# Moving every large on-chip buffer to a multiple of 512 bytes, with six stream slots set at six different offsets

## The chip, the cores and the metric

The kernel runs on one core of a Trainium2 chip. The metric is the device time of one execution in microseconds. Three runs of the kernel before took 1680.58, 1680.69 and 1686.5 us; their median is 1680.69 us.

## The reference

Attention in chunks of 64 tokens, then two feed-forward layers over the same 4608 tokens of width 512, all in float32:

```
scores = scale * (q_c @ k_c.T) ; attn = softmax(scores) ; x = attn @ v_c     # 8 x 8 x 9 chunks of 64 x 64
xn = x / sqrt(mean(x*x) + 1e-6) * rms_g
y  = (silu(xn @ w_gate) * (xn @ w_val)) @ w_out                              # 512 -> 1536 -> 512
h  = y @ w_in ;  out = (h * clip(h + 3, 0, 6) / 6) @ w_out2                  # 512 -> 2048 -> 512
```

## The kernel before

The tokens are cut into nine blocks of 512. Each value that TensorE multiplies is held as two float32r parts, a high one and a low one, and each product is three matmuls (high by high, low by high, high by low), each of a 128x128 stationary operand and a moving operand of 512 columns. Most blocks are taken in pairs with seven products in place of eight (Strassen's scheme), whose sums of operands are made once on the chip and kept in HBM.

The order of the work is written out by hand in each engine's program. There are four parts, in order of time: the start, with the attention of the first block and the preparation of the first weights; the first layer for blocks 0 to 2, one by one (`mm_up`, `mm_down_a`), with attention of later blocks spread among it (to about 360 us); the first layer for three pairs of blocks (`product` at L1032 with tiles `xu` and `wo`, `mm_down_a` with `gs` and `wd`; to about 910 us); and the second layer, one block alone and then four pairs (`product` with `xo` and `wq`, `product_down` at L1582 with `gs` and `wq`; to the end).

The operands of the second layer come from HBM through class `Stream`: 240 tiles `wq` of 128 x 1024 float32, 512 KB each, go in turn into six slots, the tags "q", "k", "qT", "kT", "p" and "v" of pool `at`. Each such tile is the stationary operand of 12 matmuls. Earlier in the kernel the same six slots hold the tiles of the attention (`Half` and `Pair`).

On-chip memory is laid out by pools in the order in which they are opened, and within a pool by tags in the order of their first use; each buffer is rounded up to 32 bytes. Before pool `const` lie 1152 bytes. Pool `const` holds `ident`, `ones`, `ones_r` (512 bytes of each partition each) and three small tiles, and ends at byte 2784. So pool `wp` (36 buffers of 4096 bytes, with weights, moving operands and results) starts at byte 2784, which is 224 past a multiple of 512. All pools after it up to `at` hold buffers of 2048, 4096 or 8192 bytes, so each of these starts 224 bytes past a multiple of 512 as well, the six slots of `at` among them. Small tiles come last, in `sm`: maxima, sums, and the tags "r" (one value of each partition, the root of the mean square) and "rc" (16 values). Each tag of `sm` has four buffers in turn.

A tile that is allocated again waits until the readers and the writer of its old content are done; the framework puts these waits on the engine that writes the new content.

The lines that matter below: L1032 in `product`, L1582 in `product_down`, L1021 in `mm_up`, L1046 to L1049 in `mm_down_a`, L1054 to L1058 in `mm_down_b`, L1782 (the last product), L656 in `heat` (matmuls of 256 columns that keep TensorE busy in the start), L650 in `pad` (64 columns), L926 in `Wide.scores` (64 columns, float32), L626 and L630 in `root` and `table`, L633 and L635 in `inv`.

Of the kernel before, what the change touches and what calls it, by code (L numbers as in the profile page):

```python
# [10 lines left out]
F32 = mybir.dt.float32  # L11
# [63 lines left out]
def fused_kernel(  # L75
# [25 lines left out]

    NQ = FB // 2
    const = ctx.enter_context(tc.tile_pool(name="const", bufs=1))
    wp = ctx.enter_context(tc.tile_pool(name="wp", bufs=36))
    xn_p = ctx.enter_context(tc.tile_pool(name="xn", bufs=1))
    xf_p = ctx.enter_context(tc.tile_pool(name="xf", bufs=1))
# [5 lines left out]
    at_p = ctx.enter_context(tc.tile_pool(name="at", bufs=1))  # L112
    sm_p = ctx.enter_context(tc.tile_pool(name="sm", bufs=4))
# [6 lines left out]
    eps = const.tile([128, 1], F32, name="eps")  # L120
    three = const.tile([128, 1], F32, name="three")
    g_sb = const.tile([128, KD], F32, name="g_sb")
    PS = ps_p.tile([128, 8, 512], F32, name="PS")
    yd = [dr_p.tile([128, KD, N], F32, name=f"yd{b}") for b in range(NB)]
    ATT, GB, VB, YB = 0, 2, 3, 4


    def w_src(kind, f):
# [370 lines left out]
    class Att:  # L499
# [22 lines left out]
        def trans_qk(self):  # L522
            ps = PS[:, self.bank:self.bank + 2, :]
            for z, t in ((0, self.q), (1, self.k)):
                if z > 0 and self.i in (0, 2):
                    self.pad()
                for a in range(NP):
                    nc.tensor.transpose(ps[:, z, a * 128:(a + 1) * 128], t[:, a * 128:(a + 1) * 128], ident)
            self.qT, self.kT = self.bufs("qT", "kT")

        def out_q(self):
            nc.scalar.copy(self.qT, PS[:, self.bank, :])

        def out_k(self):
            nc.scalar.copy(self.kT, PS[:, self.bank + 1, :])

        def scores(self):
            self.s = PS[:, self.bank:self.bank + 2, 0:256]
            ps = self.s.rearrange("p z (e c k) -> p z e c k", e=2, c=2)
            qT = self.qT.rearrange("p (a t) -> p a t", a=NP)  # L540
            kT = self.kT.rearrange("p (a t) -> p a t", a=NP)
            for a, c, j in FOURS:
                x = side(a, j)
                nc.tensor.matmul(
                    ps[x * 64:(x + 1) * 64, a // 2, a % 2, c, :],
                    qT[j * 64:(j + 1) * 64, a, c * 64:(c + 1) * 64],
                    kT[j * 64:(j + 1) * 64, a, c * 64:(c + 1) * 64],
                    start=True,
                    stop=True,
                )  # L550
# [28 lines left out]
        def trans_p(self):  # L579
            for a in range(NP):  # L580
                nc.tensor.transpose(
                    PS[:, self.bank, a * 128:(a + 1) * 128], self.p[:, a * 128:(a + 1) * 128], ident
                )
            self.pT, self.sq = self.bufs("pT", "sq")

        def out_p(self):
            nc.scalar.copy(self.pT, PS[:, self.bank, :])

# [33 lines left out]
                )  # L622

        def root(self):
            self.r = sm_p.tile([128, 1], F32, tag="r", name="r")
            nc.scalar.activation(self.r, self.ms, AF.Sqrt, scale=1.0 / DM, bias=eps)  # L626

        def table(self):
            t = sm_p.tile([128, 1], F32, tag="r", name="rt")
            nc.scalar.activation(t, eps, AF.Sqrt)  # L630

        def inv(self):
            nc.vector.reciprocal(self.r, self.r)  # L633
            self.dg = self.sq[:, 384:512]
            nc.vector.tensor_scalar(self.dg, ident, self.r, None, op0=ALU.mult)  # L635
# [310 lines left out]
    class Rms:  # L946
# [17 lines left out]

        def inv(self):
            t = at_p.tile([128, N], F32, tag="p", name="rT")
            r = sm_p.tile([128, 16], F32, tag="rc", name="rc")
            nc.vector.transpose(out=t, in_=self.rt)
            nc.vector.reciprocal(r, t.rearrange("p (j n) -> p j n", n=32)[:, :, 0])
            nc.vector.transpose(  # L970
                out=self.rt.rearrange("p (j n) -> p j n", n=32),
                in_=r.rearrange("p (j o) -> p j o", o=1).to_broadcast([128, 16, 32]),
            )
# [140 lines left out]
    with tc.manual_schedule():  # L1114
# [247 lines left out]
        for p in range(3):  # L1362
# [4 lines left out]
            def gt(f, z):  # L1367
                key = ("x", 0) if z == 0 and f < 4 else (z, f // 2)
                if key not in g:
                    g[key] = (  # L1370
                        xn_p.tile([128, KD, N], F32, tag="XL", name="ge")
                        if key == ("x", 0)
                        else wp.tile([128, 2, N], F32, tag="w", name="gu")
                    )
                return g[key][:, f % 4 if key == ("x", 0) else f % 2, :]
# [6 lines left out]
            for i in range(NI + 1):  # L1382
# [13 lines left out]
                for n, (pr, m) in enumerate(slots):  # L1396
# [19 lines left out]
                    elif (pr, m) == (3, 0):  # L1416
                        t = gt(h0, 1)
                        vec(t, t, bank(4, 0), ALU.add)
                        later = t
                    elif (pr, m) == (4, 1):  # L1420
                        t = gt(h1, 0)
# [3 lines left out]
                    elif (pr, m) == (3, 1):  # L1425
                        s = hold.pop("s2")
                        vec(s, s, bank(4, 1), ALU.add)
                        t = gt(h0, 1)
# [8 lines left out]
                    elif (pr, m) == (2, 1):  # L1437
                        t = gt(f0, 0)
                        vec(t, t, bank(0, 1), ALU.mult)
                    elif (pr, m) == (7, 0):  # L1440
                        t = gt(f1, 1)
# [3 lines left out]
                    elif (pr, m) == (7, 1):  # L1445
# [3 lines left out]
                        t = gt(f1, 1)  # L1449
# [103 lines left out]
        def slot(i, name):  # L1553

            key = (i, name)
            if key not in G:
                if i < 2 and name != "t":
                    t = xn_p.tile([128, KD, N], F32, tag=("XH", "XL")[i], name="gx")
                    names = ("11", "12", "21", "22")
                elif name == "t":  # L1560
                    t = wp.tile([128, 2, N], F32, tag="w", name="gt")
                    names = ()
                else:
                    t = wp.tile([128, 2, N], F32, tag="w", name="gu")
                    names = ("11", "12") if name[0] == "1" else ("21", "22")
                for n, x in enumerate(names):
                    G[i, x] = t[:, n, :]
                if not names:
                    for n in range(2):
                        G[i - i % 2 + n, "t"] = t[:, n, :]  # L1570
            return G[key]
# [81 lines left out]
        for b in range(1, NB, 2):  # L1653
# [7 lines left out]
            for I in range(NG + 1):  # L1661
# [7 lines left out]
                for pr, m in slots:  # L1669
# [20 lines left out]
                    elif pr == 3:  # L1690
                        t = slot(i, "12")
# [7 lines left out]
                    elif pr == 7:  # L1699
                        t = slot(i, "22")  # L1700
# [124 lines left out]
```

## Time and profile before

| | |
|---|---|
| median of three runs | 1680.69 us |
| profiled execution, its own time | 1683.83 us |
| its span, first to last instruction | 1682.0 us |
| TensorE busy | 1650.1 us (98%) |
| VectorE, ScalarE, GpSimd busy | 1086.3, 845.0, 458.7 us |
| mean granted TensorE clock | 0.994 |
| HBM traffic | 222 GB/s over the span |

The profile is of one execution, which took 3.1 us more than the median of the three runs. TensorE is busy almost throughout. A "busy" matmul lasts about 389 ns in the trace, since matmuls overlap; what one costs in a dense stretch is the stretch divided by its matmuls.

### The profile page before, as it was taken

To read this page: it belongs to the slowest core of one execution; us is meant where nothing else is said; L and a number is where in the kernel's file an instruction comes from. 1 tells how busy PE (TensorE), PEld (TensorE's weight loads), DVE (VectorE), ACT (ScalarE), POOL (GpSimd) and SP (SyncE) were. 2 spreads that over 40 slices of the span, in tenths; PEclk is the share of its full clock that TensorE was granted. 3 is DMA by queue.
4 is the path that set the end of the run, shared out by engine and by line. 5 is a ranking of instruction groups with operands and counts; after the bars stand their busy time and mean duration, and the time that the engine had idled before them with its cause. 6 is when DMAs were issued, how large, how long until landed. Compare 5 with 4: busy or idle time off the path is not lost.

```text
span 1682.0 us, 26541 instructions
## 1 busy us (share of the span) xinstructions
PE 1650.1 (98%) x9920; PEld 1352.1 (80%) x9920; DVE 1086.3 (65%) x1600; ACT 845.0 (50%) x1409; POOL 458.7 (27%) x336
## 2 busy tenths in 40 slices
PE   8999999999999999999999999999999999999998
PEld 7777788878878878788887888888788878887886
DVE  7998566656565775758436378448746764874475
ACT  6785344455454454545434344455445544654552
POOL 1001434322226522264226622131023003301310
PEclk9999999999999999999999999999999999999999
DMA  9923777748887598945979766667866786777665
GB/s 276 279 53 77 202 207 225 209 142 251 293 262 222 167 296 277 301 164 188 365 240 317 291 238 225 213 190 249 219 210 222 209 241 198 218 229 225 193 200 139
DMA packets 336096, 375.07 MB, mean 223 GB/s; under 512 B 184288, under 2 KB 260064, under 8 KB 335840
## 3 DMA queue, kind: packets, MB, share of 16 engines
q1 hardware_dynamic: 273984, 302.84, 59.6%
q10 hardware_dynamic: 61984, 70.53, 12.5%
q8 instruction: 79, 1.29, 0.3%
q14 instruction: 49, 0.40, 0.1%
HBM read 292.55 MB, written 80.74 MB: 222 GB/s over the span
## 4 chain that ended last, share of the span: by engine, by line
PE 77%; DVE 11%; DMA 5%; ACT 3%; issue 2%; SPq 2%; POOL 0%; ACTq 0%; DVEq 0%; POOLq 0%
PE PS L1032 35%; PE PS L1582 13%; PE PS L1021 9%; PE PS L1046 5%; PE PS L1049 5%; PE PS L1047 5%; DMA wo<-ops 2%; DVE gs L1576 1%; PE PS L853 1%; DVE wtmp L183 1%; DVE gt L1718 1%; PE PS L926 1%; DMA sraw<-in_moe_w_out_dram 1%; PE PS L1054 1%; PE PS L1055 1%
## 5 line engine op out<-in xcount | busy, mean ns | idle before, releaser
L1032 PE MATMUL PS<-xu,wo 128*128 128x512 f32 x1512 | 353.8, 393 | 4.8 <-DVE gu L1360 2.3
L1032 PEld LDWEIGHTS PS<-xu,wo 128*128 128x128 f32 x1512 | 283.3, 189 | 66.5 <-DVE gu L1360 3.2
L1032 PE MATMUL PS<-xo,wq 128*128 128x512 f32 x1344 | 305.3, 389 | 0.0
L1582 PE MATMUL PS<-gs,wq 128*128 128x512 f32 x1296 | 296.2, 390 | 2.4 <-DVE gs L1576 2.1
L1032 PEld LDWEIGHTS PS<-xo,wq 128*128 128x128 f32 x1344 | 252.3, 188 | 52.4
L1582 PEld LDWEIGHTS PS<-gs,wq 128*128 128x128 f32 x1296 | 242.7, 188 | 55.3 <-DVE gs L1576 5.0
L1021 PE MATMUL PS<-XH,w 128*128 128x512 f32 x576 | 149.1, 401 | 6.8 <-ACT sg L1329 4.5
L1021 PEld LDWEIGHTS PS<-XH,w 128*128 128x128 f32 x576 | 107.8, 191 | 30.7 <-ACT sg L1329 5.2
L1046 PE MATMUL PS<-gs,wd 128*128 128x512 f32 x288 | 113.4, 394 | 1.6 <-DVE gu L1360 1.6
L1047 PE MATMUL PS<-gs,wd 128*128 128x512 f32 x288 | 112.2, 389 | 0.0
L1077 POOL TENSOR_TENSOR al<-sg,ah 128x512 fp32r<-128x512 f32 x40 | 56.1, 1403 | 156.3 <-ACT ah L1075 152.1
L1356 POOL TENSOR_TENSOR gs<-gu,gs 128x512 fp32r<-128x512 f32 x60 | 86.6, 1462 | 42.4 <-ACT gs L1355 35.3
L1360 DVE TENSOR_TENSOR gu<-gu,PS 128x512 f32<-128x512 f32 x60 | 41.0, 685 | 82.2 <-ACT gu L1442 42.2
L1649 POOL TENSOR_TENSOR gt<-gx 128x512 f32<-128x512 f32 x8 | 10.3, 1289 | 299.8 <-DVE gx L1646 299.8
L1576 DVE TENSOR_TENSOR gs<-gu,gs 128x512 fp32r<-128x512 f32 x88 | 67.9, 792 | 30.9 <-ACT gs L1575 30.6
L1575 ACT CAST gs<-gt 128x512 fp32r<-128x512 f32 x96 | 58.4, 623 | 50.1 <-DVE gt L1718 44.7
L1513 DVE SCALAR_TENSOR_TENSOR gu<-gu,PS 128x512 f32<-128x512 f32 x48 | 32.8, 684 | 72.6 <-ACT gu L1510 72.6
L1021 PE MATMUL PS<-XL,w 128*128 128x512 f32 x288 | 78.2, 394 | 0.0
L1075 ACT CAST ah<-sg 128x512 fp32r<-128x512 f32 x52 | 32.3, 621 | 89.9 <-DVE sg L1333 58.0
L1049 PE MATMUL PS<-gs,wd 128*128 128x512 f32 x288 | 77.0, 389 | 0.0
L1575 ACT CAST gs<-gu 128x512 fp32r<-128x512 f32 x96 | 57.2, 621 | 22.6 <-DVE gs L1576 15.6
L1649 POOL TENSOR_TENSOR gt<-gu 128x512 f32<-128x512 f32 x24 | 32.5, 1355 | 129.1 <-DVE gu L1646 124.9
(251 smaller groups left out, 2888.9 us busy)
## 6 DMA issues: line engine op xcount, KB each, us to landing
wq<-stash_in SPq DMA_DIRECT2D x128, 512.0 KB
wo<-ops SPq DMA_DIRECT2D x126, 512.0 KB
wq<-sums_out SPq DMA_DIRECT2D x64, 512.0 KB
wq<-stash_out SPq DMA_DIRECT2D x48, 512.0 KB
wd<-keep_out SPq DMA_DIRECT2D x36, 512.0 KB
yd<-yst SPq DMA_DIRECT2D x18, 512.0 KB
ops<-w ACTq DMA_DIRECT2D x36, 256.0 KB
v<-in_v_dram SPq DMA_DIRECT2D x32, 256.0 KB
```

Source lines behind the costliest of these rows:

```text
L1021: nc.tensor.matmul(ps, w(wi, c), xs[c][xi], start=(i == 0), stop=(i == n - 1))
L1032: nc.tensor.matmul(PS[:, bank, :], op[:, wi, c * 128:(c + 1) * 128], x[xi][:, c, :], start=first and i == 0, stop=last and i == 5, skip_gr ...
L1046: nc.tensor.matmul(ps, wm[0], a[0], start=first, stop=False)
L1047: nc.tensor.matmul(ps, wm[1], a[0], start=False, stop=False)
L1049: nc.tensor.matmul(PS[:, banks[m], :], w[:, 0, m * 128:(m + 1) * 128], a[1], start=False, stop=last)
L1077: nc.gpsimd.tensor_tensor(lo, t, hi.bitcast(F32), op=ALU.subtract)
L1356: nc.gpsimd.tensor_tensor(w[:, 1, :], t, w[:, 0, :].bitcast(F32), op=ALU.subtract)
L1360: nc.vector.tensor_tensor(o, x, y, op=op)
L1575: nc.scalar.copy(w[:, 0, :], x)
L1576: e.tensor_tensor(w[:, 1, :], x, w[:, 0, :].bitcast(F32), op=ALU.subtract)
L1582: nc.tensor.matmul(PS[:, banks[m], :], op[:, wi, m * 128:(m + 1) * 128], x[xi], start=first and (wi, xi) == (0, 0), stop=False, skip_group ...
L1649: nc.gpsimd.tensor_tensor(slot(i, "t"), slot(i, "12"), slot(i, "11"), op=ALU.subtract)
```

## The change

Three edits. A tile `gap` of 24 float32 is put behind `g_sb` in `const`, and a pool `few` with two buffers a tag stands between `const` and `wp` and takes the tags "r" and "rc" from `sm`. With these, `few` starts at byte 2880 and `wp` at byte 3072, a multiple of 512. The pools after it follow: every buffer from `wp` to `tmp` now starts at a multiple of 512, where it started 224 bytes past one. Last, the six tags of `at` are touched once ahead of the program, in a fixed order, with tiles of 32 or 64 bytes between them, so that the slots "q", "k", "qT", "kT", "p", "v" start 0, 32, 64, 128, 192 and 224 bytes past a multiple of 512.

```
     const = ctx.enter_context(tc.tile_pool(name="const", bufs=1))
+    few_p = ctx.enter_context(tc.tile_pool(name="few", bufs=2))
     wp = ctx.enter_context(tc.tile_pool(name="wp", bufs=36))
...
     g_sb = const.tile([128, KD], F32, name="g_sb")
+    const.tile([128, 24], F32, name="gap")
     PS = ps_p.tile([128, 8, 512], F32, name="PS")
...
+    for n, (tag, gap) in enumerate((("q", 8), ("k", 8), ("qT", 16), ("kT", 16), ("p", 8), ("v", 0))):
+        at_p.tile([128, 2 * 512], F32, tag=tag, name=tag)
+        if gap:
+            at_p.tile([128, gap], F32, tag=f"gap{n}", name="gap")
...
         def root(self):
-            self.r = sm_p.tile([128, 1], F32, tag="r", name="r")
+            self.r = few_p.tile([128, 1], F32, tag="r", name="r")
...
         def table(self):
-            t = sm_p.tile([128, 1], F32, tag="r", name="rt")
+            t = few_p.tile([128, 1], F32, tag="r", name="rt")
...
-            r = sm_p.tile([128, 16], F32, tag="rc", name="rc")
+            r = few_p.tile([128, 16], F32, tag="rc", name="rc")
```

The touched tiles and the gaps have no instruction. On every engine the instructions are the same ones in the same order as before, with other addresses. The only waits that differ are on ScalarE in the start, where the four tiles `r` now share two buffers with `rt`. Before, ScalarE's rows there (`r` is the root of one group of 128 tokens, `xf` and `XH` hold the first block's tokens):

```order
L626 ACTIVATE r<-PS,eps 128x1 [waits PE_49]
L612 COPY xf<-PS 128x2x4x64 [waits PE_49]
L615 ACTIVATE pT<-PS 128x2x4x64
L194 CAST w<-wraw 128x512 [waits DVE_49]
L626 ACTIVATE r<-PS,eps 128x1 [waits PE_49]
L659 CAST XH<-xf 128x4x128 [waits DVE_49,Activation_49]
L626 ACTIVATE r<-PS,eps 128x1 [waits PE_49,Activation_49]
```

The same rows of ScalarE after the change (each line number is 7 higher):

```order
L633 ACTIVATE r<-PS,eps 128x1 [waits PE_49,Activation_49]
L619 COPY xf<-PS 128x2x4x64 [waits PE_49]
L622 ACTIVATE pT<-PS 128x2x4x64
L201 CAST w<-wraw 128x512 [waits DVE_49]
L633 ACTIVATE r<-PS,eps 128x1 [waits DVE_49,PE_49]
L666 CAST XH<-xf 128x4x128 [waits DVE_49]
L633 ACTIVATE r<-PS,eps 128x1 [waits PE_49]
```

Nothing moved. The second root now also waits for ScalarE's own write to `rt`, and the third for VectorE's last reading of the first root, since each takes over a buffer.

## Rows read from the trace of the kernel before

**Rows 1.** The page: busy time of the engines, DMA's share, the chain by engine.
```profile
PE 1650.1 (98%) x9920; PEld 1352.1 (80%) x9920; DVE 1086.3 (65%) x1600; ACT 845.0 (50%) x1409; POOL 458.7 (27%) x336
...
DMA packets 336096, 375.07 MB, mean 223 GB/s; under 512 B 184288, under 2 KB 260064, under 8 KB 335840
...
PE 77%; DVE 11%; DMA 5%; ACT 3%; issue 2%; SPq 2%; POOL 0%; ACTq 0%; DVEq 0%; POOLq 0%
```

**Rows 2.** Chain that ended last, by pieces: start us, us, what.
```profile
441.44 16.55 PE PS L1032 x72
...
489.02 4.93 PE PS L1032 x11
...
1058.88 76.16 PE PS L1032 x336
...
1135.04 54.19 PE PS L1582 x239
```

**Rows 3.** Busy time by stretches: us, engines (instructions), granted clock, DMA share, GB/s.
```profile
441.50:457.90 16.40, 16.40 (x73) 13.52 (x74) 10.77 (x14) 9.89 (x14) 6.13 (x4) 1.00 0.96 354
1059.00:1135.00 76.00, 76.00 (x337) 62.96 (x336) 31.84 (x47) 36.74 (x60) 20.63 (x16) 1.00 0.66 203
...
487.00:493.70 6.70, 6.70 (x76) 5.58 (x76) 2.00 (x2) 1.75 (x3) 0.76 (x1) 0.50 0.72 233
```

**Rows 4.** Groups of matmuls: count, then busy us, mean ns, idle before.
```profile
L1032 PE MATMUL PS<-xu,wo 128*128 128x512 f32 x1512 | 353.8, 393 | 4.8 <-DVE gu L1360 2.3 <-ACT gu L1442 1.1 <-DVE s L1360 0.9
L1032 PE MATMUL PS<-xo,wq 128*128 128x512 f32 x1344 | 305.3, 389 | 0.0
L1582 PE MATMUL PS<-gs,wq 128*128 128x512 f32 x1296 | 296.2, 390 | 2.4 <-DVE gs L1576 2.1
L1021 PE MATMUL PS<-XH,w 128*128 128x512 f32 x576 | 149.1, 401 | 6.8 <-ACT sg L1329 4.5 <-ACT XH L659 2.2
...
L1021 PE MATMUL PS<-XL,w 128*128 128x512 f32 x288 | 78.2, 394 | 0.0
L1049 PE MATMUL PS<-gs,wd 128*128 128x512 f32 x288 | 77.0, 389 | 0.0
...
L1021 PE MATMUL PS<-xr,wq 128*128 128x512 f32 x192 | 46.0, 389 | 0.0
L1049 PE MATMUL PS<-al,w 128*128 128x512 f32 x144 | 38.5, 389 | 0.0
...
L1058 PE MATMUL PS<-w,al 128*128 128x512 f32 x64 | 17.1, 389 | 0.0
L1782 PE MATMUL PS<-gs,wq 128*128 128x512 f32 x48 | 13.2, 434 | 2.5 <-DMA wq<-stash_out 2.5
```

**Rows 5.** What TensorE waited for: us in total, times, longest.
```profile
PE PS L1021 <- ACT sg L1329: 4.5, 2, 3.2
PE PS L596 <- ACT pT L587: 2.8, 6, 0.7
PE PS L1782 <- DMA wq<-stash_out: 2.5, 1, 2.5
PE PS L1032 <- DVE gu L1360: 2.3, 1, 2.3
```

**Rows 6.** Chain again: two runs of 64-column matmuls.
```profile
6.19 1.07 PE PS L650 x16
...
397.09 1.09 PE PS L926 x64
```

**Rows 7.** DMA queues, 1188.4 to 1192.4 us: packets, MB, share of 16 engines.
```profile
q1 hardware_dynamic: 3851, 0.48, 81.4%
```

**Rows 8.** DMA queues, 400 to 420 us: packets, MB, share of 16 engines.
```profile
q1 hardware_dynamic: 1373, 4.49, 72.4%
q10 hardware_dynamic: 544, 0.52, 7.5%
```

**Rows 9.** ScalarE and VectorE in order of time: start us, us, instruction.
```profile
24.47 0.20 ACT L630 ACTIVATE rt<-eps 128x1 f32<-128x1 f32 x1
...
27.58 0.31 ACT L626 ACTIVATE r<-PS,eps 128x1 f32<-128x1 f32 x1
...
29.72 0.27 ACT L626 ACTIVATE r<-PS,eps 128x1 f32<-128x1 f32 x1
...
27.46 0.29 DVE L635 TENSOR_SCALAR pT<-ident,r 128x128 f32<-128x128 f32 x1
```

## The prediction

> **What bounds the kernel now.** I read the page first. TensorE is busy for 1650.1 of 1682.0 us, and 77% of the chain that ended last is TensorE's own work [rows 1]. The list of its waits then shows that what is not busy is small: its longest entries are 4.5, 2.8, 2.5 and 2.3 us [rows 5], and all its gaps together are 1682.0 - 1650.1 = 31.9 us. So a change pays only if it changes what one matmul costs, or adds or takes a good part of those 32 us.
>
> Next, the pieces of the chain, for the cost of one matmul. In the second layer 336 matmuls of L1032 take 76.16 us without a break: 226.67 ns each. A piece that follows other work carries a lead of about 0.23 us (16.55 us for 72, less 72 x 226.67 ns = 16.32 us) [rows 2]. L1582, with other tiles, gives 54.19 / 239 = 226.7 ns [rows 2]. So the cost is one number all over the kernel. Once the clock is at the lower level (granted 0.50, which is 1.2 GHz) [rows 3]: there 11 matmuls take 4.93 us, less the lead 4.70 us or 427 ns each [rows 2]. 512 columns at 1.2 GHz are 426.7 ns, so nothing is added at that level. At 2.4 GHz they are 213.33 ns, and the row says 226.67: every matmul carries 13.33 ns beyond its columns. I call it the bubble.
>
> How many matmuls carry it? The groups of 512 columns [rows 4] are 1512 + 1344 + 1296 + 576 + 288 + 192 + 48, plus L1046, L1047 and L1049 with 288 (`gs`) and 144 (`ah`, `al`) each and L1054, L1055 and L1058 with 64 each (of these triples the last stands for all): 6,744. The bubble is 6,744 x 13.33 ns = 89.9 us of the run. It is the only sizable thing that an address could touch.
>
> **The change part by part.** It removes and adds no instruction. Three things differ.
>
> *The new waits.* The second root (27.58 us) waits for ScalarE's own write to `rt`, over at 24.47 + 0.20 = 24.67 us. The third (29.72 us) waits for VectorE's last reading of the first root, over at 27.46 + 0.29 = 27.75 us, 1.97 us earlier [rows 9]. Cost 0; the cover is those 1.97 us. Were it gone, the cast of `XH` and the last root stand behind that root on ScalarE, and the first matmuls of the first layer wait for them. To cost 1 us the reading would have to be 3 us late. The tag "rc" is used by VectorE alone, in order: 0.
>
> *Transfers.* Buffers move from 224 bytes past a multiple of 512 to 0, and the six slots to 0, 32, 64, 128, 192, 224. In a stretch of only small packets, 3,851 packets of 125 bytes use 81.4% of 16 engines over 4.0 us: 0.814 x 16 x 4000 / 3851 = 13.5 ns each [rows 7]. The stores on q10 between 400 and 420 us are 956 bytes each and take 0.075 x 16 x 20000 / 544 = 44.1 ns; the loads on q1 there are 3,270 bytes and take 168.7 ns [rows 8]. The first two give 30.6 ns for 831 bytes, or 0.0368 ns a byte, and 13.5 - 125 x 0.0368 = 8.9 ns that every packet pays. All of these touch buffers at 224, so no row separates a part due to the address. Bounds: at best all 8.9 ns of a 168.7 ns load goes, 5.3%; the chain is on DMAs for 5% of 1682 us = 84 us [rows 1], so this gives -4.5 us. At worst packets lengthen by as much: a landing late by 5.3% costs +4.5 us in the earlier parts, and nothing in the second layer, where 336 and 239 matmuls run through without a wait for a tile [rows 2] at a DMA share of 0.66 [rows 3]. I take 0, since start 224 is present in every row from 125 to 3,270 bytes and the same 8.9 ns fits them without an address.
>
> *The matmuls.* Moving and stationary operands both start 224 bytes past a multiple of 512 now. After, the moving ones start at 0, stationary `w`, `wo`, `wd` and `gs` at 0, and `wq` at one of six offsets. No row of before shows another start for a 512-column matmul. The nearest rows are the 64-column runs: L650 reads `ones` for both operands, 128 bytes past a multiple of 512, and L926 reads `qT` and `kT`, 224 past one. 16 of the first take 1.07 us; 64 of the second, which run four side by side in the array (so 16 passes), take 1.09 us [rows 6]. That is 67 and 68 ns a pass: no price for the start. They are float32 and pass at a slower rate, so they don't settle it. Bounds for one 512-column matmul: 213.33 ns from below, what its columns need; from above one more bubble, 240 ns. I take 226.67, the value of every dense piece, because a fixed cost of each matmul that the lower clock hides needs no address to explain it.
>
> Between engines, one rule bears on this. The Trainium skill, "SBUF — State Buffer", section "SBUF: two separate sides", says that DMA ports and engine ports are apart and that TensorE and ScalarE never wait on another user of the memory. Here the trace agrees: at a DMA share of 0.96 the 72 matmuls from 441.44 us cost the same as the 336 at 0.66 [rows 2, 3]. By that rule no placement of the slots against the transfers can change the matmuls, and the sum stays at 0.
>
> VectorE, ScalarE and GpSimd read and write the moved buffers too. No row shows a price by address for them. TensorE's waits for them are a part of 31.9 us, so even 10% on all their operations is at most 3 us either way.
>
> **The sum.** 0 + 0 + 0. The profiled execution took 1683.83 us, its span 1682.0; the three runs' median of 1680.69 lies 3.1 us below. Against the median I forecast 1680.5 us. Adding the small bounds (4.5 and 3 us each way), the likeliest case lies between 1673 and 1688 us. A measurement of this kernel tells no less than 0.5%, 8.4 us, from no change.
>
> **The rivals.**
>
> *A: the bubble comes from where the moving operand starts.* Then it goes everywhere, since all moving operands now start at 0: 1680.7 - 89.9 = 1591 us. For it: 13.33 ns at 4 bytes a column is the time of 32 columns, or 128 bytes, the size of a piece that is read too much when the start is odd; and it is hidden at the lower clock, as a reading cost would be. Against it: the 64-column rows. Chance 0.06. The Trainium skill, "TensorE: Matmul & The Clock Gate", section "Wait — 56ns, not 53.3ns?", gives N/2.4 GHz plus about 2.5 ns back to back, 215.8 ns for 512 columns. The trace disagrees by 10.9 ns a matmul; by that rule, as an estimate, 73 us of the bubble is a loss of this kernel, and rival A would end near 1607 us.
>
> *B: the bubble comes from both operands starting at the same place*, so that the reading of the next stationary operand and of the moving one collide. It would go where they differ: in the second layer, 1344 + 1296 + 192 + 48 = 2,880 matmuls (12 a tile, 240 tiles), for the five slots of six that are not at 0: 2,400 x 13.33 ns = 32.0 us, 1649 us. If only some offsets help, 6.4 us for each such slot. For it: all dense rows have equal starts and all have the bubble. Against it: the reading of a 128-column operand is a quarter as long as that of 512 columns, and a collision would not cost exactly the same in 336 and in 239 matmuls with different tiles. Chance 0.11, a third of it for one to three slots.
>
> *C: slower.* Unequal starts are what collides, and equal starts are the free case. The place is the second layer; the price is one more bubble on 2,400 matmuls, +32 us, 1713 us; it decides from 8.4 us / 2,400 = 3.5 ns a matmul. One bad slot costs 6.4 us, two 12.8. For it: before, no dense matmul has unequal starts, so it is untried. Against it: the same row that speaks against B. Chance 0.10, half of it for one or two slots.
>
> *D: the shift does less than it says*, since the slots also serve the attention, whose tiles are written in pieces; there only the transfers could feel it, and that is in the bounds above.
>
> **How the numbers follow.** No effect 0.73, A 0.06, B 0.11, C 0.10. The time is that of the first, 1680.5 us. Its own range is 1673 to 1688. To leave out no more than 2 in 10, the range goes to 1660 below (three slots of B) and 1695 above (two slots of C); outside are A, two thirds of B and half of C, 0.18. Faster by over 0.5%: A and most of B, 0.16. Slower: C without its single-slot case, and a little for transfers, 0.10. Within: 0.74.
>
> **What would show it.** In the chain after, the 336 matmuls of L1032 still take 76.16 us; 71.7 would be A, 72.4 B, 79.9 C, and B or C would show as a cost that changes from tile to tile, every 12 matmuls, in a pattern of six. The 72 matmuls near 441 us tell A from B: under A they fall to 15.6 us, under B they stay. The lead-in around 30 us shows the waits. A clock that is granted differently, or a wait for `wq` in the second layer, would make the forecast wrong in a way that I give no price.

## The result, and the profile after

The changed kernel takes 1693.29 us (median of 5 runs, 1691.22 to 1695.04); the kernel before, run beside it, 1681.07 us. The ratio is 1.0071, 95% interval 1.0057 to 1.0084: 12 us slower. The forecast of no change was wrong. The time lies inside the stated range, but in the part that was there for rival C, which had a chance of 0.10.

The profiled execution has a span of 1693.2 us, 11.2 us more than before. First the page of the changed kernel: busy time by engine, then the chain that ended last (start us, us, what; every line number is 7 higher than before).

```profile
PE 1663.0 (98%) x9920; PEld 1351.1 (80%) x9920; DVE 1088.0 (64%) x1600; ACT 845.1 (50%) x1409; POOL 460.2 (27%) x336
```

```profile
1060.41 77.85 PE PS L1039 x336
...
1216.91 77.89 PE PS L1039 x336
...
1373.44 77.94 PE PS L1039 x336
...
1530.01 77.86 PE PS L1039 x336
1607.88 61.13 PE PS L1589 x264
```

TensorE is 12.9 us longer busy; VectorE, ScalarE and GpSimd differ by 1.7 us or less [rows 1]. The 336 matmuls that took 76.16 us [rows 2] take 77.85 to 77.94 us. L1589 has 61.13 / 264 = 231.6 ns a matmul, where 226.7 ns stood [rows 2]. Now the groups of matmuls: count, busy us, mean ns, idle before.

```profile
L1039 PE MATMUL PS<-xu,wo 128*128 128x512 f32 x1512 | 354.4, 393 | 4.5 <-DVE gu L1367 2.3 <-ACT gu L1449 0.9 <-DVE s L1367 0.9
L1039 PE MATMUL PS<-xo,wq 128*128 128x512 f32 x1344 | 312.2, 394 | 0.0
L1589 PE MATMUL PS<-gs,wq 128*128 128x512 f32 x1296 | 302.2, 394 | 1.1 <-DVE gs L1583 0.8
L1028 PE MATMUL PS<-xr,wq 128*128 128x512 f32 x192 | 46.9, 394 | 0.0
L1056 PE MATMUL PS<-al,w 128*128 128x512 f32 x144 | 38.5, 389 | 0.0
L1789 PE MATMUL PS<-gs,wq 128*128 128x512 f32 x48 | 11.8, 398 | 2.2 <-DMA wq<-stash_out 2.2
```

The three large groups that read `wq` have grown, from a mean of 389 or 390 ns to 394 ns [rows 4]; the groups of the first layer, with both operands in `wp` (or moving ones in `al`), keep their old means within 1 ns. The 72 matmuls near 441 us, which the prediction named as a sign, take 16.62 us in order of time, before as after. So the loss is in the second layer, among the matmuls whose stationary operand lies in a shifted slot. Within the changed kernel the slots can be told apart. The chain over the first six tiles of a product, one row a tile; the slots start 192, 224, 0, 32, 64 and 128 bytes past the start of the moving operands:

```profile
1060.41 2.75 PE PS L1039 x12
1063.16 2.79 PE PS L1039 x12
1065.96 2.73 PE PS L1039 x12
1068.68 2.79 PE PS L1039 x12
1071.48 2.80 PE PS L1039 x12
1074.27 2.79 PE PS L1039 x12
```

The third row, distance 0, is the cheapest: 2.73 / 12 = 227 ns, close to the 226.67 of before (12 of those are 2.72 us). The others cost 229 (192) to 233 ns. That is the pattern of six that the prediction named as the sign of B or C, with the sign of C.

The sum of the parts: the four runs of 336 give 311.54 - 4 x 76.16 = 6.9 us; L1589 1296 x 4.7 ns = 6.1 us (231.4 in its 49.76 us for 215 between other work); L1028 0.9 us; together 13.9. Two things took 2.7 us off, which leaves 11.2, the difference of the two spans (all else differs by some tenths of a us). L1589 waited 0.8 us for `gs`, where it waited 2.1. That goes with the dearer matmuls, which give the other engines more time: in the two kernels below whose slots cost nothing this wait is 2.4 and 2.0 us, and 0.2 us in the dearest one. And the last 48 matmuls are busy for 11.8 us, not 13.2 [rows 4], since more of them ran at the upper clock: the granted clock of the last 20 us is 0.96, before 0.90. This second part does not come from the change, for the kernel below with all slots at 256 bytes, where no matmul is dearer, has 11.6 us there.

The new waits cost nothing that shows: the two roots of the start begin at 27.50 and 29.60 us, where they began at 27.58 and 29.72 us before [rows 9].

### The profile page after: what moved, and what is told of

Its sections match the earlier page's. It is cut to its first block, busy times and chain, and to the rows that moved or that the text cites. A ratio compares the mean times of both kernels' runs of the same rounds, so it can differ in the third digit from the quotient of the medians.

```text
span 1693.2 us, 26541 instructions
## 1 busy us (share of the span) xinstructions
PE 1663.0 (98%) x9920; PEld 1351.1 (80%) x9920; DVE 1088.0 (64%) x1600; ACT 845.1 (50%) x1409; POOL 460.2 (27%) x336
## 4 chain that ended last, share of the span: by engine, by line
PE 46%; DVE 5%; DMA 1%; issue 1%; ACT 0%; SPq 0%; DVEq 0%; POOL 0%; ACTq 0%; POOLq 0%
PE PS L1039 24%; PE PS L1589 13%; PE PS L1028 3%; DVE gs L1583 2%; PE PS L1056 1%; PE PS L1053 1%; PE PS L1054 1%; PE PS L1061 1%; PE PS L1062 1%; PE PS L1065 1%; DVE gt L1725 1%; DVE oq L1603 1%; PE PS L1789 1%; DMA stash_in<-sc 1%; DVE xo L1508 0%
## 5 line engine op out<-in xcount | busy, mean ns | idle before, releaser
L1039 PE MATMUL PS<-xo,wq 128*128 128x512 f32 x1344 | 312.2, 394 | 0.0
L1589 PE MATMUL PS<-gs,wq 128*128 128x512 f32 x1296 | 302.2, 394 | 1.1 <-DVE gs L1583 0.8
L1589 PEld LDWEIGHTS PS<-gs,wq 128*128 128x128 f32 x1296 | 243.0, 188 | 59.6 <-DVE gs L1583 3.6
L1028 PE MATMUL PS<-XH,w 128*128 128x512 f32 x576 | 149.3, 402 | 7.0 <-ACT sg L1336 4.7
L1028 PEld LDWEIGHTS PS<-XH,w 128*128 128x128 f32 x576 | 107.8, 191 | 30.9 <-ACT sg L1336 5.4
L1656 POOL TENSOR_TENSOR gt<-gx 128x512 f32<-128x512 f32 x8 | 10.4, 1296 | 305.2 <-DVE gx L1653 304.6
L1028 PE MATMUL PS<-XL,w 128*128 128x512 f32 x288 | 78.1, 393 | 0.0
```

What stands on the lines that cost most here:

```text
L1028: nc.tensor.matmul(ps, w(wi, c), xs[c][xi], start=(i == 0), stop=(i == n - 1))
L1039: nc.tensor.matmul(PS[:, bank, :], op[:, wi, c * 128:(c + 1) * 128], x[xi][:, c, :], start=first and i == 0, stop=last and i == 5, skip_gr ...
L1589: nc.tensor.matmul(PS[:, banks[m], :], op[:, wi, m * 128:(m + 1) * 128], x[xi], start=first and (wi, xi) == (0, 0), stop=False, skip_group ...
L1656: nc.gpsimd.tensor_tensor(slot(i, "t"), slot(i, "12"), slot(i, "11"), op=ALU.subtract)
```

## The experiments

In what follows, the distance is the start of the stationary operand less the start of the moving one, in bytes. Theory 1 is rival C made precise: the reading of the moving operand and of the stationary one hinder each other unless both start at the same place modulo some power of two. Theory 2: multiples of 512 are dear in themselves. Theory 3: the slots' own starts, or the transfers into them, make the cost.

**The slots without gaps.** Everything, the slots too, at multiples of 512.

```
-    for n, (tag, gap) in enumerate((("q", 8), ("k", 8), ("qT", 16), ("kT", 16), ("p", 8), ("v", 0))):
+    for n, (tag, gap) in enumerate((("q", 0), ("k", 0), ("qT", 0), ("kT", 0), ("p", 0), ("v", 0))):
```

> The change without the gaps between the six slots: every large buffer, the slots too, starts at a multiple of 512. Theory 1 (unequal starts): a 512-column matmul costs 226.67 ns where its stationary and moving operands start at the same place modulo 512, and some 230 to 234 ns where not. Then the 336 matmuls of the second layer take 76.2 us again, and the time is that of before, 1681 us (1678 to 1684). Theory 2 (multiples of 512): moving operands that start at a multiple of 512 are the dearer ones, whatever the slots do. Then the 336 matmuls stay near 77.85 us and the time near 1693 us.

Measured: 1678.67 us (12 runs) against 1681.42; ratio 0.9986, interval 0.9974 to 0.9999. Its chain:

```profile
1058.23 76.16 PE PS L1039 x336
```

The loss is gone, so multiples of 512, the pool `few` and the new waits cost nothing: they are all still here. Theory 2 falls, and with it rival A: all moving operands start at a multiple of 512, and the 13.33 ns remain.

**The gaps alone.** The pools stay at 224, the slots are shifted against them.

```
-    few_p = ctx.enter_context(tc.tile_pool(name="few", bufs=2))
     wp = ctx.enter_context(tc.tile_pool(name="wp", bufs=36))
...
     sm_p = ctx.enter_context(tc.tile_pool(name="sm", bufs=4))
+    few_p = ctx.enter_context(tc.tile_pool(name="few", bufs=2))
...
-    const.tile([128, 24], F32, name="gap")
```

> The other half alone: all pools stay 224 bytes past a multiple of 512 as before the change (the pool of small tiles goes to the end), and the six slots get the gaps of the change, so that they start 0, 32, 64, 128, 192 and 224 bytes past where the moving operands start. Theory 1 (only the distance between the two operands counts): the same cost slot by slot as in the changed kernel, 336 matmuls in 77.6 to 78.1 us, time 1691 to 1695 us. Theory 2 (multiples of 512 are dear for the moving operand): 76.2 us and 1681 us. Theory 3 (some absolute starts of the slot are dear, 32, 64, 128, 192 and 224 past a multiple of 512): here the slots start at 224, 256, 288, 352, 416 and 448, so the pattern over the six tiles must change and the slot at distance 0 (start 224) must be one of the dear ones.

Measured: 1693.25 us, ratio 1.0076 (1.0056 to 1.0096), the whole loss.

```profile
1058.49 77.85 PE PS L1038 x336
```

Slots at 224, 256, 288, 352, 416 and 448 cost what those at 0 to 224 did: only the distance between the operands counts, not where a slot lies. Theory 3's first half falls.

**Other distances.** The slots at 0, 96, 160, 256, 288, 320, and then at 0, 128, 384, 416, 448, 480 bytes. The edit of the first:

```
-    const.tile([128, 24], F32, name="gap")
...
-    for n, (tag, gap) in enumerate((("q", 8), ("k", 8), ("qT", 16), ("kT", 16), ("p", 8), ("v", 0))):
+    for n, (tag, gap) in enumerate((("q", 24), ("k", 16), ("qT", 24), ("kT", 8), ("p", 8), ("v", 0))):
```

The second is without the gap in `const` too, and has gaps of 32, 64, 8, 8, 8 and 0 values and three buffers a tag in `sm`.

> As the change, but the slots at distances 0, 96, 160, 256, 288 and 320 bytes from the start of the moving operands (all modulo 512; the moving ones start 416 past a multiple of 512). Theory 1: the slot at distance 0 costs 226.67 ns a matmul, the others more. If what counts repeats every 256 bytes, the slot at 256 costs 226.67 ns too, and 288 and 320 cost what 32 and 64 did, 232.6 and 233.1 ns. If it repeats only at 512 or not at all, all five are dear, 229 to 234 ns, and the 336 matmuls take 77.5 to 78.2 us. If the cost fell with distance, the slot at 256 would be the cheapest of the five.

> As the change, but the slots at distances 0, 128, 384, 416, 448 and 480 bytes (moving ones 416 past a multiple of 512; the small tiles have three buffers a tag in place of four, for room). Theory 1: distance 0 costs 226.67 ns, 128 the 232.7 ns that it cost in the changed kernel, and the other four show the rest of the circle. If a repeat at 256 bytes holds, 384, 448 and 480 equal 128, 192 and 224 (232.7, 229.7, 232.7 ns). If only the nearness to a multiple of 512 counts, 480 and 32 are alike, and 448 and 64.

Measured, one run each: 1691.18 and 1692.82 us. Tiles of the first at distances 0, 160, 256, and of the second at 480, 384, 416, each a row of its chain:

```profile
1060.92 2.75 PE PS L1038 x12
...
1066.49 2.79 PE PS L1038 x12
1069.28 2.77 PE PS L1038 x12
```

```profile
1061.10 2.79 PE PS L1038 x12
...
1069.40 2.79 PE PS L1038 x12
1072.20 2.80 PE PS L1038 x12
```

480 costs what 224 did, 384 what 128 did, 416 what 160 did (288, 320 and 448, with 2.79, 2.79 and 2.75 us, fit what 32, 64 and 192 did). That spoke for a repeat every 256 bytes, but 256 itself (2.77 us, 231 ns) was not free, and in the first of the two, distance 0 was not either (2.75 us, 229 ns). So this was open: is it the distance that costs, or the change of distance from tile to tile? Three more runs were for that.

**Six slots at one distance.** All at 256, and all at 64.

```
+    at_p.tile([128, 64], F32, tag="lead", name="gap")
-    for n, (tag, gap) in enumerate((("q", 8), ("k", 8), ("qT", 16), ("kT", 16), ("p", 8), ("v", 0))):
+    for n, (tag, gap) in enumerate((("q", 0), ("k", 0), ("qT", 0), ("kT", 0), ("p", 0), ("v", 0))):
```

(16 values instead of 64 for the second. The first is without the gap in `const`, for room.)

> As the change, but all six slots at one distance of 256 bytes from the start of the moving operands. If the pattern repeats every 256 bytes: the 336 matmuls take 76.2 us and the time is 1679 to 1682 us, as with equal starts. If it repeats only every 512: 77.5 us or more and 1690 us or more.

> As the change, but all six slots at a distance of 64 bytes, the dearest of the six that the change has (233.1 ns in undisturbed tiles). Theory 1 with a cost by distance: all 2,880 matmuls of the second layer cost 6.4 ns more than at equal starts, 18 us, less some 1 us of waits that they cover: 1695 to 1699 us, and 78.3 us for the 336 matmuls. If it is the change of distance from tile to tile that costs (a rhythm that is lost and found again) and not the distance, a common distance is free: 76.2 us and 1681 us.

Measured: at 256 1680.94 us, ratio 0.9997 (0.9982 to 1.0012); at 64 1695.93 us, ratio 1.0079 (1.0050 to 1.0108). Their chains:

```profile
1056.14 76.16 PE PS L1039 x336
```

```profile
1057.64 78.40 PE PS L1040 x336
```

A distance of 256 is as free as 0, so the pattern repeats every 256 bytes, as far as these distances show. A common distance of 64 costs 78.40 / 336 = 233.3 ns a matmul throughout, so the distance itself costs; nothing has to change from tile to tile.

**The matmuls by themselves.** Groups of 48 matmuls without a transfer of data, with two loops over a table of starts in place of the kernel (it computes nothing of the reference):

```
+                o = (dw, swing - dw)[i % 2 if swing else 0] // 4 + (0 if same else i % 6) * 128
+                m = (dm, swing - dm)[i % 2 if swing else 0] // 4 + i // 2 % 4 * 512
+                nc.tensor.matmul(PS[0:wide, i % 2, 0:cols], W[name][:, o:o + wide], mv[:, m:m + cols], start=True, stop=True)
```

> A kernel that computes nothing of the reference: groups of 48 back-to-back matmuls of the kind of the second layer (128x128 stationary, 512 columns moved, float32r), each group with its own start of the two operands, no transfer under way and no other engine at work from the third group on. Theory 1 (the two readings of TensorE collide): the costs of the big kernel come back without any transfer: 226.7 ns at distance 0, 232 to 234 ns at 32, 64, 96, 128, 160 and 224 bytes, 230 ns at 192; 320 like 64. Theory 3 (transfers that write into the slots collide with the readings): all groups cost 226.7 ns. At 256 bytes: 226.7 ns if the pattern repeats every 256 bytes, 232 or more if every 512. With both operands moved by 32: 226.7 ns by theory 1. If it is the stationary operand of the next matmul that is read while a matmul runs, the group in which each matmul has equal starts but its successor has not (starts 0,0 then 64,64) is dear, and the one with unequal starts in each matmul but the next one's stationary equal to the present moving one (0,64 then 64,0) costs 226.7 ns; if a matmul's own two operands collide, it is the other way round. At 64 columns of stationary operand the extra cost of unequal starts should halve at least; at 256 moved columns it should stay the same per matmul.

TensorE in order of time; from one row's start to the next row's is the cost of 48:

```profile
22.15 11.05 PE L115 MATMUL PS<-mv,wda 128*128 128x512 f32 x48
33.03 11.32 PE L115 MATMUL PS<-mv,wdb 128*128 128x512 f32 x48
44.19 11.23 PE L115 MATMUL PS<-mv,wdc 128*128 128x512 f32 x48
...
77.65 11.36 PE L115 MATMUL PS<-mv,wdf 128*128 128x512 f32 x48
88.85 11.40 PE L115 MATMUL PS<-mv,wdg 128*128 128x512 f32 x48
100.09 11.32 PE L115 MATMUL PS<-mv,wdh 128*128 128x512 f32 x48
...
122.45 11.16 PE L115 MATMUL PS<-mv,wdj 128*128 128x512 f32 x48
133.44 11.36 PE L115 MATMUL PS<-mv,wdk 128*128 128x512 f32 x48
144.64 11.04 PE L115 MATMUL PS<-mv,wdl 128*128 128x512 f32 x48
155.52 11.36 PE L115 MATMUL PS<-mv,wdm 128*128 128x512 f32 x48
166.72 11.10 PE L115 MATMUL PS<-mv,wea 128*128 128x512 f32 x48
177.66 11.36 PE L115 MATMUL PS<-mv,web 128*128 128x512 f32 x48
188.85 5.92 PE L115 MATMUL PS<-mv,wfa 128*128 128x256 f32 x48
194.61 5.82 PE L115 MATMUL PS<-mv,wfb 128*128 128x256 f32 x48
200.26 11.20 PE L115 MATMUL PS<-mv,wga 128*64 128x512 f32 x48
211.30 11.34 PE L115 MATMUL PS<-mv,wgb 128*64 128x512 f32 x48
222.47 11.36 PE L115 MATMUL PS<-mv,wha 128*128 128x512 f32 x48
233.67 11.30 PE L115 MATMUL PS<-mv,wka 128*128 128x512 f32 x48
244.80 11.28 PE L115 MATMUL PS<-mv,wkb 128*128 128x512 f32 x48
255.92 11.04 PE L115 MATMUL PS<-mv,wdz 128*128 128x512 f32 x48
```

Distance 0 (`wda`): (33.03 - 22.15) / 48 = 226.7 ns. 4 bytes (`wdb`): 232.5. 64 (`wdf`): 233.3. 96 (`wdg`): 234.2. 192 (`wdj`): 229.0. 256 (`wdl`): 226.7. With both operands moved by 32 bytes (`wea`): 227.9 (of this more in the last section), and with the moving one alone (`web`): 233.1. So the costs come back with no transfer under way and, from the third group on, no other engine at work. Theory 3 falls whole: the cost arises within TensorE and hangs on its two operands' starts. That it is their two readings that collide is the natural account, but no run here looks inside.

Three expectations did not come out as meant. Each second matmul of `wka` and `wkb` has other starts. In `wka` each matmul's two operands start alike, but the next one's stationary operand starts elsewhere; in `wkb` the moving operand and the next matmul's stationary one start alike, and a matmul's own two do not. Both are dear (231.9 and 231.7 ns), so neither pair of starts alone makes the cost. With 64 columns of stationary operand the step from distance 0 to 64 did shrink, from 6.6 to 2.7 ns, but only because distance 0 itself is dear there: 230.0 ns (`wga`), against 232.7 at 64 (`wgb`). And with 256 columns moved, distance 64 is the cheaper one: 117.7 (`wfb`) against 120.0 ns (`wfa`). Reading the same stationary tile each time, at distance 64, is no cheaper: 233.3 ns (`wha`).

**Other kinds of operand.** The same, with two-byte operands (`wqa` to `wqd`), 384 columns (`wna`, `wnb`), 256 columns at five distances and 32 columns of stationary operand (`wsa`, `wsb`); nothing of the reference is computed.

```
+    mb = big.tile([128, 4 * 512], BF, name="mb")
+    nc.scalar.copy(mb, raw[:, 0:2048])
...
+                nc.tensor.matmul(PS[0:wide, i % 2, 0:cols], W[name][:, o:o + wide], (mb if two else mv)[:, m:m + cols], start=True, stop=True)
```

> Groups of 48 matmuls by themselves again, nothing of the reference computed, to see what the 13.3 ns beyond the columns hang on that stay at equal starts. If they are a matter of reading (4 bytes a column in both operands), two-byte operands (bfloat16) lose them: 512 columns near 216 ns, 256 near 109, and a distance of 64 or 128 bytes costs nothing there. If they are a fixed cost of every matmul, bfloat16 pays them too: 226.7 and 120 ns. Float32r at 384 columns: 160 + 13.3 = 173.3 ns at equal starts. At 256 columns, where a distance of 64 bytes was cheaper (117.8 against 120.0 ns), a lower cost at 32, 128 and 192 bytes too would show that equal starts are best only for 512 columns. A stationary operand of 32 columns should lose both the 13.3 ns and the extra cost if the reading of the stationary operand makes them.

```profile
36.09 10.53 PE L117 MATMUL PS<-mb,wqa 128*128 128x512 bf16 x48
46.47 10.52 PE L117 MATMUL PS<-mb,wqb 128*128 128x512 bf16 x48
56.83 10.52 PE L117 MATMUL PS<-mb,wqc 128*128 128x512 bf16 x48
...
73.30 7.62 PE L117 MATMUL PS<-mv,wna 128*128 128x384 f32 x43
80.75 8.64 PE L117 MATMUL PS<-mv,wnb 128*128 128x384 f32 x48
89.23 5.84 PE L117 MATMUL PS<-mv,wma 128*128 128x256 f32 x48
...
117.67 11.28 PE L117 MATMUL PS<-mv,wsa 128*32 128x512 f32 x48
128.79 11.29 PE L117 MATMUL PS<-mv,wsb 128*32 128x512 f32 x48
139.91 11.06 PE L117 MATMUL PS<-mv,wdz 128*128 128x512 f32 x48
```

In bfloat16 a matmul of 512 columns costs (56.83 - 46.47) / 48 = 215.8 ns at a distance of 64 bytes, and as much at 128. At distance 0 it is (46.47 - 36.09) / 48 = 216.3 ns with the change from float32r at the group's start. So the distance costs nothing, and 2.5 ns stand beyond the columns in place of 13.3: of the two types tried, both costs belong to float32r alone.

At 384 columns the rule of 512 holds, by less: 173.3 ns at distance 0 (the last 43 of `wna`: 7.45 us), 176.7 at 64 (`wnb`). At 256 columns it is turned round: 120.0 ns at distance 0, 118.3 at 32, 118.5 at 128, 117.7 at 192 and 117.9 at 64. With 32 columns of stationary operand the cost does not fall: 231.7 ns at distance 0 and at 64, against the expectation. What exactly collides is therefore not settled by these runs.

No kernel is clearly faster than the one before. The one without gaps is 0.14% faster, its interval just below 1.

## Why the prediction was wrong

*What bounds the kernel, and the 13.33 ns.* Right: the loss is TensorE's cost per matmul (13.9 us, of which 11.2 are left in the span).

*The new waits, 0.* Right: the experiment without gaps has them and is not slower.

*The transfers, 0 within 4.5 us.* Right in size: with everything at multiples of 512 the ratio is 0.9986, or 2.4 us less, inside the bound whatever makes it. One reading was wrong: the line through the two smaller packets gives 8.9 + 3,270 x 0.0368 = 129 ns for the loads, and the row says 168.7, so "the same 8.9 ns fits them" does not hold and was no support for the 0.

*The matmuls, 0.* Wrong, and this is the step that failed: "I take 226.67, the value of every dense piece, because a fixed cost of each matmul that the lower clock hides needs no address to explain it." All dense pieces had equal starts, so their one value said nothing of unequal starts; it was the value at the best place. Worse, a sentence ahead of it in the same paragraph, "No row of before shows another start for a 512-column matmul", does not hold for the trace of before. The mean of squares (L960, L961) multiplies `ones_r`, 128 bytes past a multiple of 512, with `sqh`, 224 past one, 16 matmuls in all. In the trace of before (min/median/max ns):

```profile
L960 PE MATMUL PS<-sqh,ones_r x8: 394/394/398, 142.2 to 770.1; 128*128 128x512 f32 x8
L961 PE MATMUL PS<-sqh,ones_r x8: 393/393/501, 142.8 to 770.3; 128*128 128x512 f32 x8
```

At their shortest 394 and 393 ns, where the groups of `wq` have 389 or 390 on average [rows 4]: about the same 5 ns that the `wq` groups show after. As an estimate, 2,880 x 5 ns = 14.4 us, less the 2.7 us above, is near the loss.

*TensorE's waits for the other engines, 0 within 3 us.* Right: all its gaps together went from 31.9 to 1693.2 - 1663.0 = 30.2 us.

*The 64-column rows, as evidence against a price.* They were no evidence: float32 matmuls, which the prediction itself called slower, and their operands had equal starts in both rows.

*The rule that ports of transfers and engines are apart.* This is what the prediction took from the Trainium skill ("SBUF — State Buffer", section "SBUF: two separate sides"). Between transfers and TensorE the runs agree with it: 226.7 ns at distance 0 and 233.3 at 64, in the kernel and with no transfer under way. But the loss needs no second user of the memory, so the argument could not speak for the 0.

*Rival A.* Refuted. The 215.8 ns of the Trainium skill ("TensorE: Matmul & The Clock Gate", section "Wait — 56ns, not 53.3ns?") are what bfloat16 measures here; float32r measures 226.7 at its best, and no placement tried here came below that. The bubble stays where all operands start at multiples of 512.

*Rival B.* Its sign was wrong: at 512 columns, equal starts are the free case. Its counter-argument, that the reading of 128 columns is a quarter as long as that of 512, had no row behind it. The traces have 188 ns for one load of 128 float32r columns, 134 of 64 and 109 of 32. By the difference of the first two, an estimate, 128 columns take 108 ns, half of the 213 of a matmul's 512.

*Rival C.* Right in place and sign: "Unequal starts are what collides, and equal starts are the free case." The runs show the second half; the collision stays the natural account. Its price, one more bubble of 13.33 ns on 2,400 matmuls, was more than twice too high: 13.9 us on 2,400 are 5.8 ns, and the five distances of the change cost 2.3 ns (192) to 6.7 ns (64 and 224) by themselves. Its reason for the low chance, "the same row that speaks against B", was weak, because that row could not speak of starts either.

*The range.* That 1693.29 us lies inside it is luck. Its upper end was set by two bad slots of C at 6.4 us each; in fact all five were bad, each at half of that price or less.

## What to carry to other kernels

Where every dense row shares a property, their agreement says nothing of a change to that property; look for the odd instruction, however short, that lacks it (here 16 matmuls about 5 ns longer). For 512-column float32r matmuls with 128 stationary columns, start moving and stationary operands at the same place modulo 256 bytes: a common base and tiles in multiples of 256 do that, and a small tile put between two pools can undo it. For other widths measure it: at 384 columns equal starts were still best, at 256 they were the worst.

## What the runs showed of the hardware

At equal starts the steady cost can come back with a delay after a group at another distance. The group `wea` costs 227.9 ns on average: its first 8 matmuls take 1.86 us, 232.5 ns each, the other 40 from the row below to 177.66 us, 227.0 ns.

```profile
168.58 9.24 PE L115 MATMUL PS<-mv,wea 128*128 128x512 f32 x40
```

The group at 256 (`wdl`) shows no such delay. A delay of this kind would explain why, in the mixed kernels with 12 matmuls a tile, the tiles at distance 0 cost 227 to 229 ns and the one at 256 costs 231 ns, though alone it costs 226.7; the delay's own cause is open.

A distance of only 4 bytes costs almost as much as one of 64 (232.5 and 233.3 ns). At distance 0 float32r matmuls carry 13.3 ns beyond their columns at 2.4 GHz, at 512, 384 and 256 columns alike (226.7, 173.3, 120.0 ns), bfloat16 2.5 ns at 512; why is open.
